# Pooled attention and a top-1 mixture of experts on one core: one last scatter, an early drain of POOL, gathers behind their test, and undivided second tiles

## The chip, the cores and the metric

The kernel runs on one core of one Trainium2 chip. The core has five engines, each with an instruction queue of its own: TensorE (PE in the profile, with PEld for its weight loads), VectorE (DVE), ScalarE (ACT), GpSimd (POOL) and SyncE (SP, which issues most DMAs). POOL issues the indirect DMAs: gathers and scatters of rows by an index per partition. The metric is the device time of one execution in microseconds, the median over several.

## The reference

The inputs are `q`, `k`, `v` of 8 batches x 8 heads x 576 positions x 64, a modality id for each of the 4608 tokens, a gate matrix 512x8, a bias per modality, and the experts' weights `w1` (8 x 512 x 1024) and `w2` (8 x 1024 x 512), all in float32. Cut to what matters:

```python
k_p = k.reshape(B, H, S // 8, 8, D).mean(axis=3); v_p = ...          # pooled by 8
attn = softmax(q @ k_p.T / sqrt(D)) @ v_p
x = attn.transpose(0, 2, 1, 3).reshape(B * S, H * D)                 # 4608 tokens x 512
logits = x @ w_gate + modality_bias[modality_id]
e_idx = argmax(logits); gate_w = softmax(logits)[e_idx]
for e in range(E):                                                    # each token goes to one expert
    mask = e_idx == e
    out[mask] = gate_w[mask, None] * (relu(x[mask] @ w1[e]) @ w2[e])
```

## The kernel before, in words

**Attention.** Tokens are worked on in 36 tiles of 128, in 20 steps of two tiles (`z` = 0 and 1) or one "mixed" tile. The tiles form four groups of nine; groups 0 and 1 are early, 2 and 3 late (`EARLY_GROUPS`). `x_dve` (L603) ends a tile: PSUM tile `av` holds for each head the weighted sum of values and, in a last column, the sum of weights. DVE takes the sums (L620), their reciprocals (L622) and the logits' share (L624), then writes the row `xo` of the tile into `xw` (xb in the profile). An early tile is divided on DVE, in two halves of 256 columns (L626 and L631). A late tile is divided on DVE in its upper half only (L626); ACT copies the lower half as it is (L629), and the reciprocals go into eight further columns of the row (`RX`). SP stores the rows to `xs` in DRAM, where a row has 512 + 16 columns: the token's vector, its gate, and the eight factors, which are 1 for rows that are divided already. `av` has a single buffer, so PE can start the next tile's product only when DVE and ACT have read it. Further small steps of the routing are "dripped" between DVE's instructions (`gap`).

**Experts.** Tokens are sorted by expert into slots of 256 (two tiles of 128). A slot belongs to one expert; the number of slots depends on the data and is 18 to 27 (`NSTAT` to `NSLOT`). Slots 0 and 1 take tokens from the early groups and are prepared during the attention. For each slot:

- POOL gathers its rows from `xs` (`gather`, L141, two indirect DMAs into `xg`), multiplies the lower half of each tile by its factors (`scale_half`, L148, the product at L152), PE transposes the tiles (`x_transposes`, L155, the transposes at L161), ACT and DVE split the result into a high and a low part (L163, L164).
- For `f` in 0 to 7, an eighth of the hidden units: `hidden(f)` is 12 matmuls into `hp` (L170), with ReLU on ACT (L172) and the low part on DVE (L174); `second(f)` is 6 matmuls into `op` (L1155). `renew(f)` splits the next slot's weights: high part on ACT (L136), low part on DVE, a subtraction 128x1024 from two SBUF operands (L139), after which SP loads the weights of the slot after that.
- `evac` (L1132) multiplies `op` by the gate, tile 0 on DVE (L1137), tile 1 on ACT (L1139), and POOL scatters both tiles to `out` (L1141). A scatter waits for the landing of the one before it.

`run` (L1188) writes the order out by hand. In slot s, at `f` = 0 stand `evac` of slot s - 1 (`tail`) and the gather of slot s + 1, at `f` = 3 the factors' product, at `f` = 5 the transposes for slot s + 1; at the end of `f` = 7 the first hidden step of the next slot. Slot 1 differs: its gather is at `f` = 3, the product at 5, the transposes at 6, because the indices of slot 2 are only computed in slots 0 and 1 (`late`, L1103: the table's product and the five DVE steps that finish it, L763 to L767, stand at slot 1, `f` = 2).

**The end.** The number of slots is read into a register in all engines. From slot 17 (`NSTAT` - 1) on, after `f` = 2 (`CUT` = 3), a test decides whether a further slot follows (`more`, L1267, the test at L1280). If it does, the slot is finished by `run`, the next slot's first three steps follow, and so on, nested. If not, `end` or `end_half` (L1222, L1236, chosen by a test at L1272) finishes the slot without preparing another; `end_half` does so when the last slot has only one tile of tokens. On a path that skips DMAs, the POOL queue waits for those in flight and accounts for the skipped ones, so that the semaphores agree where the paths meet (`EVENT_SEMAPHORE` and `INC_SWDGE_SEM` at L1280). `last_rows` (L1215) writes the last rows to `obl[0]` (DVE) and `obl[1]` (ACT); `end_half` sets `obl[1]` to zero, and its indices lie outside of `out`. Behind all tests stand two scatters (L1289), `obl[1]` first. L1317 is the end of the program, with a DRAIN on every engine.

With these inputs 19 slots are used, 0 to 18; slot 18 has one tile and takes `end_half`. The gather of slot 19 that stands at `f` = 0 of slot 18 is issued, and nobody reads it.

Of the kernel before, what the change touches and what calls it, by code (L numbers as in the profile page):

```python
# [12 lines left out]
I32 = mybir.dt.int32  # L13
# [17 lines left out]
def kernel(  # L31
# [116 lines left out]
    def scale_half(s, xgs):  # L148
        for tt in range(2):
            x = xgs[(2 * s + tt) % len(xgs)]  # L150
            xv = x[:, 0:D // 2].rearrange("p (h d) -> p h d", h=H // 2)
            nc.gpsimd.tensor_tensor(xv, xv, x[:, RX:RX + H // 2].rearrange("p (h o) -> p h o", o=1).to_broadcast([P, H // 2, HD]),  # L152
                                    op=ALU.mult)
# [37 lines left out]
    with ExitStack() as actx:  # L191
# [411 lines left out]
        def x_dve(t):  # L603
# [5 lines left out]
            if gi == 0:  # L609
# [7 lines left out]
            late = g >= EARLY_GROUPS  # L617
# [8 lines left out]
            nc.vector.tensor_tensor(xo[:, D // 2:D].rearrange("p (h d) -> p h d", h=4),  # L626
                                    avv[:, 1, :, 0:HD], rb[:, 1].to_broadcast([P, 4, HD]), op=ALU.mult)
            if late:
                nc.scalar.copy(xo[:, 0:D // 2].rearrange("p (h d) -> p h d", h=4), avv[:, 0, :, 0:HD])  # L629
# [495 lines left out]
    def part(s):  # L1125
# [6 lines left out]
        def evac(tts=(0, 1)):  # L1132
            for tt in tts:
                ob = mp.tile([P, D], F32, tag="ob", bufs=4, name=f"ob_{s}_{tt}")
                gt = xg[(2 * s + tt) % 4][:, D:D + 1]
                if tt == 0:
                    nc.vector.tensor_scalar_mul(ob, o[tt], gt)  # L1137
# [3 lines left out]
                nc.gpsimd.indirect_dma_start(  # L1141
                    out=out[:, :], out_offset=IndirectOffsetOnAxis(idx.bitcast(U32), 0),
                    in_=ob, in_offset=None, bounds_check=NTOK - 1, oob_is_err=False)
# [44 lines left out]
        def run(fs, tail):  # L1188
            for f in fs:
# [11 lines left out]
                if s == 1 and f == 3:  # L1201
# [13 lines left out]
        def last_rows(tt):  # L1215
            gt = xg[(2 * s + tt) % 4][:, D:D + 1]
            if tt == 0:
                nc.vector.tensor_scalar_mul(obl[0], o[0], gt)
            else:
                nc.scalar.activation(obl[1], o[1], AF.Copy, scale=gt)  # L1220

        def end(f0):  # L1222

            nc.vector.tensor_copy(sl, sidx[:, 2 * s:2 * s + 2])
# [6 lines left out]
            last_rows(1)  # L1231
            for f in range(f0, NF):
                second(f, (0,), at[f])
            last_rows(0)

        def end_half(f0):  # L1236

            nc.vector.tensor_copy(sl, sidx[:, 2 * s:2 * s + 2])
            nc.vector.memset(obl[1], 0.0)
# [6 lines left out]
            last_rows(0)  # L1246
# [6 lines left out]
    obl = [mp.tile([P, D], F32, name=f"obl{z}") for z in range(2)]  # L1253
    sl = mp.tile([P, 2], I32, name="sl")
# [33 lines left out]
    for tt in (1, 0):  # L1288
        nc.gpsimd.indirect_dma_start(  # L1289
            out=out[:, :], out_offset=IndirectOffsetOnAxis(sl[:, tt:tt + 1].bitcast(U32), 0),  # L1290
            in_=obl[tt], in_offset=None, bounds_check=NTOK - 1, oob_is_err=False)
# [30 lines left out]
```

## Time and profile before

| | us |
|---|---|
| median of 3 runs | 634.19 (633.3 to 634.3) |
| profiled execution | 631.66 |
| its span, first to last instruction | 629.9 |
| PE busy | 601.1 (95%) |
| DVE busy | 409.1 (65%) |
| ACT busy | 347.6 (55%) |
| POOL busy | 237.8 (38%) |

The granted clock of TensorE is 0.992 in the mean. The attention lasts until about 187 us, slot 1 runs from about 198 to 221, slot 18 begins at about 600, PE's last matmul ends at 617.8. A busy share alone says little here; what can be gained is read from the stretches in which PE is idle and from what ends that idle time. In the rows, a time in square brackets is the idle time of the engine ahead of the instruction, followed by what ended it; `x18 | 7.4, 413 |` means 18 instructions, 7.4 us in all, 413 ns each.

### The profile page before, as it was taken

How to read it: one execution, taken by the hardware profiler on the slowest of the kernel's cores; microseconds unless marked ns; L12 is line 12 of the kernel's file. 1: busy time of each engine (PE TensorE's matmuls, PEld its weight loads, DVE VectorE, ACT ScalarE, POOL GpSimd, SP SyncE). 2: the span in 40 equal slices, each digit the busy share in tenths (PEclk: the TensorE clock that was granted, in tenths of full speed). 3: DMA queues.
4: the chain of work that ended last, by engine and by line, in shares of the span. 5: the costliest groups of instructions: out<-in, count | busy, mean ns of one | idle time of the engine just before them, and what ended most of it. 6: DMA issues, size and time to landing. Idle time of an engine off the chain costs nothing.

```text
span 629.9 us, 12488 instructions
## 1 busy us (share of the span) xinstructions
PE 601.1 (95%) x4223; PEld 544.8 (86%) x4223; DVE 409.1 (65%) x802; ACT 347.6 (55%) x666; POOL 237.8 (38%) x326
## 2 busy tenths in 40 slices
PE   4799999999999999999999999999999999999992
PEld 3699888897898898999999999999999999999991
DVE  4767888778957487656656566566566656656641
ACT  2667677887532555555555555555555555555540
POOL 5789968742000341331332331331331241331331
PEclk9899999999999999999999999999999999999997
DMA  9999969864113620120220460120135310120120
GB/s 252 308 284 350 355 199 362 261 209 137 53 70 110 227 69 17 52 69 7 64 69 16 153 223 31 50 68 18 53 91 183 132 56 18 53 69 18 52 70 19
DMA packets 63481, 77.12 MB, mean 122 GB/s; under 512 B 15535, under 2 KB 42159, under 8 KB 63408
## 3 DMA queue, kind: packets, MB, share of 16 engines
q1 hardware_dynamic: 57168, 55.98, 28.2%
q0 software_dynamic: 6240, 20.26, 10.0%
q8 instruction: 35, 0.57, 0.4%
q14 instruction: 38, 0.31, 0.2%
HBM read 119.94 MB, written 19.71 MB: 222 GB/s over the span
## 4 chain that ended last, share of the span: by engine, by line
PE 78%; DMA 6%; DVE 5%; issue 4%; ACT 3%; SPq 1%; POOL 1%; POOLq 0%; ACTq 0%; DVEq 0%
PE op L1155 29%; PE hp L170 29%; PE av L597 5%; PE sc L533 4%; PE av L601 2%; PE xt L161 2%; PE pq L508 2%; DMA out_dram<-ob,sidx 2%; PE pp L562 1%; PE ph L170 1%; DMA xg<-xs,gidx 1%; DMA k<-in_k_dram 1%; DMA raw<-in_moe_w_dram 1%; DVE kp L309 1%; DVE sb L543 1%
## 5 line engine op out<-in xcount | busy, mean ns | idle before, releaser
L136 ACT CAST hl<-raw 128x1024 fp32r<-128x1024 f32 x138 | 144.8, 1049 | 138.7 <-PE op L1155 134.7
L170 PE MATMUL hp<-xh,hl 128*128 128x256 f32 x1152 | 186.1, 284 | 0.0
L170 PEld LDWEIGHTS hp<-xh,hl 128*128 128x128 f32 x1152 | 166.1, 189 | 10.5
L139 DVE TENSOR_TENSOR hl<-raw,hl 128x1024 fp32r<-128x1024 f32 x144 | 175.0, 1217 | 0.0
L1155 PE MATMUL op<-hl,hh 128*128 128x512 f32 x554 | 173.5, 394 | 0.0
L1141 POOL DMA_INDIRECT out_dram<-ob,sidx x36 | 52.5, 1457 | 289.6 <-DVE ob L1137 184.5
L174 DVE SCALAR_TENSOR_TENSOR hlo<-hp,hh 128x256 fp32r<-128x256 f32 x139 | 58.7, 423 | 136.4 <-ACT hh L172 123.8
L1155 PE MATMUL op<-hl,hlo 128*128 128x512 f32 x277 | 108.4, 391 | 0.0
L1155 PEld LDWEIGHTS op<-hl,hh 128*128 128x128 f32 x554 | 94.8, 189 | 12.1
L170 PE MATMUL hp<-xl,hl 128*128 128x256 f32 x576 | 92.0, 282 | 0.0
L172 ACT ACTIVATE hh<-hp 128x256 fp32r<-128x256 f32 x139 | 53.3, 383 | 49.7 <-PE hp L170 47.8
L170 PEld LDWEIGHTS hp<-xl,hl 128*128 128x128 f32 x576 | 79.0, 190 | 0.0
L1155 PEld LDWEIGHTS op<-hl,hlo 128*128 128x128 f32 x277 | 52.0, 188 | 11.7
L597 PE MATMUL av<-vw,pt 128*128 128x146 f32 (+1 forms) x320 | 50.4, 297 | 1.4 <-ACT pt L567 0.9
L143 POOL DMA_INDIRECT xg<-xs,gidx x40 | 44.2, 1105 | 16.5 <-issue 10.4
L152 POOL TENSOR_TENSOR xg<-xg 128x256 f32<-128x256 f32 x34 | 31.2, 918 | 34.9 <-DMA xg<-xs,gidx 34.9
L597 PEld LDWEIGHTS av<-vw,pt 128*128 128x128 f32 (+1 forms) x320 | 40.3, 182 | 3.8 <-ACT pt L567 2.3
L533 PE MATMUL sc<-kt,qt 128*128 128x144 f32 x256 | 38.0, 292 | 0.0
L164 DVE TENSOR_TENSOR xl<-xt,xh 128x512 fp32r<-128x512 f32 x38 | 24.6, 685 | 17.1 <-ACT xh L163 17.1
L533 PEld LDWEIGHTS sc<-kt,qt 128*128 128x128 f32 x256 | 34.2, 195 | 0.2
L540 DVE TENSOR_REDUCE mx<-sc 128x8 f32<-128x576 f32 (+1 forms) x40 | 27.7, 692 | 10.0 <-PE sc L533 8.3
L601 PE MATMUL av<-vw,pt 128*128 128x146 f32 (+1 forms) x160 | 30.7, 295 | 0.4
(236 smaller groups left out, 713.0 us busy)
## 6 DMA issues: line engine op xcount, KB each, us to landing
raw<-in_moe_w_dram SPq DMA_DIRECT2D x304, 256.0 KB
xs<-xb SPq DMA_DIRECT2D x16, 528.0 KB
k<-in_k_dram SPq DMA_DIRECT2D x7, 1024.0 KB
v<-in_v_dram SPq DMA_DIRECT2D x7, 1024.0 KB
q<-in_q_dram SPq DMA_DIRECT2D x6, 1024.0 KB
q<-in_q_dram SPq DMA_DIRECT2D x4, 512.0 KB
v<-in_v_dram SPq DMA_DIRECT2D x16, 128.0 KB
xs<-xb SPq DMA_DIRECT2D x8, 132.0 KB
```

The costliest lines, as they stand in the source:

```text
L136: nc.scalar.copy(hl[f][:, 0, :], raw[f])
L139: eng.tensor_sub(hl[f][:, 1, :], raw[f], hl[f][:, 0, :].bitcast(F32))
L143: nc.gpsimd.indirect_dma_start(out=xgs[(2 * s + tt) % len(xgs)], out_offset=None, in_=xs[0:rows, :], in_offset=IndirectOffsetOnAxis(idx[:, ...
L152: nc.gpsimd.tensor_tensor(xv, xv, x[:, RX:RX + H // 2].rearrange("p (h o) -> p h o", o=1).to_broadcast([P, H // 2, HD]), op=ALU.mult)
L170: nc.tensor.matmul(ph, hl[f][:, w, d * P:(d + 1) * P], x[:, d, :], start=(n == 0 and d == 0), stop=(n == 2 and d == ND - 1))
L172: nc.scalar.activation(hh, ph, AF.Relu)
L174: nc.vector.scalar_tensor_tensor(hlo, ph, 0.0, hh.bitcast(F32), op0=ALU.max, op1=ALU.subtract)
L533: nc.tensor.matmul(dst, qt[:, i, :], kt[b % NB][:, :, h * SPL:(h + 1) * SPL], start=True, stop=True)
L597: nc.tensor.matmul(av[hs, u, 2 * VC * gg:2 * VC * (gg + 1)], pt[:, c, hs], vw[y][:, c].rearrange("p a x -> p (a x)"), start=(gg == 0), sto ...
L601: nc.tensor.matmul(dst4[hs], pt4[:, hs], v4[y][:, 2 * u:2 * u + 2, :], start=False, stop=True)
L1141: nc.gpsimd.indirect_dma_start(out=out[:, :], out_offset=IndirectOffsetOnAxis(idx.bitcast(U32), 0), in_=ob, in_offset=None, bounds_check=N ...
L1155: nc.tensor.matmul(o[tt], l[:, ts_], hl[f][:, w, D:2 * D], start=(f == 0 and n == 0), stop=(f == NF - 1 and n == 2))
```

## The change

- `scale_half` becomes `scale`: POOL multiplies all 512 columns of both tiles, not 256.
- In `x_dve` only second tiles (`z` = 1) of the late groups leave undivided, and they do so whole: one copy 128x512 on ACT, nothing on DVE. First tiles and mixed tiles of the late groups are divided on DVE in two halves, as the early ones are.
- In slot 1 the two scatters of slot 0's rows are put off (`later`) until behind the product for slot 2; slot 2's gather moves from `f` = 3 to `f` = 2, its product from 5 to 4.
- From slot 17 on, the gather of the next slot moves from `f` = 0, ahead of the test, to `f` = 3, behind it; the product moves from 3 to 4, the transposes from 5 to 6.
- In slot 16, at `f` = 4, behind the product for slot 17, POOL gets a `drain`.
- There is one scatter behind all tests. `end` scatters its second tile itself, through `evac`; the first tile, or the only one, is multiplied by the gate half on DVE and half on ACT and goes out by the one last scatter. `end_half` no longer sets a second tile to zero.

```diff
-    def scale_half(s, xgs):
+    def scale(s, xgs):
...
-            xv = x[:, 0:D // 2].rearrange("p (h d) -> p h d", h=H // 2)
-            nc.gpsimd.tensor_tensor(xv, xv, x[:, RX:RX + H // 2].rearrange("p (h o) -> p h o", o=1).to_broadcast([P, H // 2, HD]),
+            xv = x[:, 0:D].rearrange("p (h d) -> p h d", h=H)
+            nc.gpsimd.tensor_tensor(xv, xv, x[:, RX:RX + H].rearrange("p (h o) -> p h o", o=1).to_broadcast([P, H, HD]),
...
-            late = g >= EARLY_GROUPS
+            late = g >= EARLY_GROUPS and z == 1
...
-            nc.vector.tensor_tensor(xo[:, D // 2:D].rearrange("p (h d) -> p h d", h=4),
-                                    avv[:, 1, :, 0:HD], rb[:, 1].to_broadcast([P, 4, HD]), op=ALU.mult)
             if late:
-                nc.scalar.copy(xo[:, 0:D // 2].rearrange("p (h d) -> p h d", h=4), avv[:, 0, :, 0:HD])
+                nc.scalar.copy(xo.rearrange("p (u h d) -> p u h d", u=2, h=4), avv[:, :, :, 0:HD])
             else:
-                nc.vector.tensor_tensor(xo[:, 0:D // 2].rearrange("p (h d) -> p h d", h=4),
-                                        avv[:, 0, :, 0:HD], rb[:, 0].to_broadcast([P, 4, HD]), op=ALU.mult)
+                for u in range(2):
+                    nc.vector.tensor_tensor(xo[:, u * D // 2:(u + 1) * D // 2].rearrange("p (h d) -> p h d", h=4),
+                                            avv[:, u, :, 0:HD], rb[:, u].to_broadcast([P, 4, HD]), op=ALU.mult)
...
                 if f == 0:
-                    tail()
-                    if nxt and s >= EARLY_SLOTS:
+                    if s == 1:
+                        tail(later=later)
+                    else:
+                        tail()
+                    if nxt and EARLY_SLOTS <= s < NSTAT - 1:
                         gather(s + 1, gidx, 2 * (s + 1), xg)
...
-                if s == 1 and f == 3:
+                if s == 1 and f == 2:
+                    gather(s + 1, gidx, 2 * (s + 1), xg)
+
+                if s >= NSTAT - 1 and f == CUT and nxt:
                     gather(s + 1, gidx, 2 * (s + 1), xg)
...
-                if f == (5 if s == 1 else 3) and nxt and not early:
-                    scale_half(s + 1, xg)
-                if f == (6 if s == 1 else 5) and nxt:
+                if f == (3 if EARLY_SLOTS <= s < NSTAT - 1 else 4) and nxt and not early:
+                    scale(s + 1, xg)
+                    while later:
+                        later.pop(0)()
+                if s == NSTAT - 2 and f == 4:
+                    nc.gpsimd.drain()
+                if f == (5 if EARLY_SLOTS <= s < NSTAT - 1 else 6) and nxt:
                     x_transposes(s + 1, xg)
...
+        def last_rows():
+
+            gt = xg[2 * s % 4][:, D:D + 1]
+            nc.vector.tensor_scalar_mul(obl[:, 0:D // 2], o[0][:, 0:D // 2], gt)
+            nc.scalar.activation(obl[:, D // 2:D], o[0][:, D // 2:D], AF.Copy, scale=gt)
...
-            last_rows(1)
+            evac((1,))
             for f in range(f0, NF):
                 second(f, (0,), at[f])
-            last_rows(0)
+            last_rows()
...
-            nc.vector.memset(obl[1], 0.0)
...
-    for tt in (1, 0):
-        nc.gpsimd.indirect_dma_start(
-            out=out[:, :], out_offset=IndirectOffsetOnAxis(sl[:, tt:tt + 1].bitcast(U32), 0),
-            in_=obl[tt], in_offset=None, bounds_check=NTOK - 1, oob_is_err=False)
+    nc.gpsimd.indirect_dma_start(
+        out=out[:, :], out_offset=IndirectOffsetOnAxis(sl.bitcast(U32), 0),
+        in_=obl, in_offset=None, bounds_check=NTOK - 1, oob_is_err=False)
```

More of the change, by code (lines that the diff above doesn't have):

```diff
@@ L1130, in part, with evac @@
         early = s + 1 < EARLY_SLOTS
-        def evac(tts=(0, 1)):
+        def evac(tts=(0, 1), later=None):
             for tt in tts:
@@ L1140, in evac, with put @@
                 idx = (sidx0 if s < EARLY_SLOTS else sidx)[:, 2 * s + tt:2 * s + tt + 1]
-                nc.gpsimd.indirect_dma_start(
-                    out=out[:, :], out_offset=IndirectOffsetOnAxis(idx.bitcast(U32), 0),
-                    in_=ob, in_offset=None, bounds_check=NTOK - 1, oob_is_err=False)
+                def put(ob=ob, idx=idx):
+                    nc.gpsimd.indirect_dma_start(
+                        out=out[:, :], out_offset=IndirectOffsetOnAxis(idx.bitcast(U32), 0),
+                        in_=ob, in_offset=None, bounds_check=NTOK - 1, oob_is_err=False)
+                if later is None:
+                    put()
+                else:
+                    later.append(put)
         def hidden(f, at=None):
@@ L1188, in run @@
         def run(fs, tail):
+            later = []
             for f in fs:
@@ L1192, in run @@
                 if f == 0:
-                    tail()
-                    if nxt and s >= EARLY_SLOTS:
+                    if s == 1:
+                        tail(later=later)
+                    else:
+                        tail()
+                    if nxt and EARLY_SLOTS <= s < NSTAT - 1:
                         gather(s + 1, gidx, 2 * (s + 1), xg)
@@ L1213, in run @@
                     renew(f)
[L1215 to L1220, printed above, removed]
+        def last_rows():
+            gt = xg[2 * s % 4][:, D:D + 1]
+            nc.vector.tensor_scalar_mul(obl[:, 0:D // 2], o[0][:, 0:D // 2], gt)
+            nc.scalar.activation(obl[:, D // 2:D], o[0][:, D // 2:D], AF.Copy, scale=gt)
         def end(f0):
-            nc.vector.tensor_copy(sl, sidx[:, 2 * s:2 * s + 2])
+            nc.vector.tensor_copy(sl, sidx[:, 2 * s:2 * s + 1])
             at = {f: hx[f - f0] for f in range(f0, NF)}
@@ L1230, in end @@
             second(NF - 1, (1,), at[NF - 1])
-            last_rows(1)
+            evac((1,))
             for f in range(f0, NF):
                 second(f, (0,), at[f])
-            last_rows(0)
+            last_rows()
         def end_half(f0):
-            nc.vector.tensor_copy(sl, sidx[:, 2 * s:2 * s + 2])
-            nc.vector.memset(obl[1], 0.0)
+            nc.vector.tensor_copy(sl, sidx[:, 2 * s:2 * s + 1])
             at = {f: hx[f - f0] for f in range(f0, NF)}
@@ L1245, in end_half @@
             second(NF - 1, (0,), at[NF - 1])
-            last_rows(0)
+            last_rows()
         return slot0 if s == 0 else run, end, evac, end_half
@@ L1251 @@
     hx = [[mp.tile([P, SLOT], F32R, name=f"hx{i}_{z}") for z in range(2)] for i in range(NF - CUT)]
-    obl = [mp.tile([P, D], F32, name=f"obl{z}") for z in range(2)]
-    sl = mp.tile([P, 2], I32, name="sl")
+    obl = mp.tile([P, D], F32, name="obl")
+    sl = mp.tile([P, 1], I32, name="sl")
     lag = []
```

2 lines of the change are left out of this document (1 added, 1 removed).

## The prediction

> **What bounds the kernel now.** I read first the busy time by stage, to see where TensorE (PE) is not the bound. Columns: stretch, its length, then busy us and instructions of PE, weight loads, DVE, ACT, POOL, the granted clock, DMA share and GB/s.
>
> ```profile
> 90.00:187.00 97.00, 94.31 (x788) 86.03 (x787) 75.88 (x228) 66.19 (x183) 39.59 (x62) 1.00 0.59 191
> 218.00:578.00 360.00, 360.00 (x2363) 327.74 (x2364) 225.81 (x308) 197.24 (x291) 104.11 (x90) 1.00 0.21 68
> 618.00:630.00 12.00, 0.00 (x0) 0.00 (x0) 0.61 (x1) 0.00 (x0) 1.92 (x2) 0.69 0.07 23
> ```
>
> From 218 to 578 PE has no idle time, so nothing can be won there; things can only be lost. What is to be won lies in three places: 2.69 us of idle PE in the late attention (97.00 less 94.31), one wait at slot 1, and 12 us at the end in which PE does nothing. The waits of PE name the first two, and the waits of ACT one more:
>
> ```profile
> PE xt L161 <- ACT qt L514: 1.0, 1, 1.0
> PE xt L161 <- POOL xg L152: 0.7, 1, 0.7
> ACT xb L629 <- DVE xb L626: 8.9, 8, 2.2
> ```
>
> The third place I read in the timeline of the last microseconds, in the chain of waits that ends last (start, length, what), and in the instructions of two lines (L1280 is the slot test, L1317 the end of the program; three numbers are min/median/max in ns, then first and last start):
>
> ```profile
> 616.22 1.60 PE L1155 MATMUL op<-hl,hx 128*128 128x512 f32 x6
> 617.86 0.75 DVE L1218 TENSOR_SCALAR obl<-op,xg 128x512 f32<-128x512 f32 x1 [0.60 <-PE op L1155]
> 617.91 1.01 POOL L1289 DMA_INDIRECT out_dram<-obl,sl  x1 [8.62 <-DVE hx L174]
> 621.63 1.00 POOL L1289 DMA_INDIRECT out_dram<-obl,sl  x1 [2.71 <-DMA out_dram<-obl,sl]
> ```
> ```profile
> 614.31 2.54 issue
> ...
> 617.91 2.94 DMA out_dram<-obl,sl
> ```
> ```profile
> L1280 POOLq EVENT_SEMAPHORE  x5: 17/43/5426, 606.7 to 612.5; - x5
> L1280 POOLq INC_SWDGE_SEM  x1: 1699/1699/1699, 612.5 to 612.5; - x1
> ```
> ```profile
> L1317 SPq DRAIN  x3: 7/7/13, 624.9 to 629.4; - x3
> L1317 POOLq DRAIN  x3: 40/113/7685, 621.4 to 629.7; - x3
> ```
>
> The rows to publish are ready at 618.61 (617.86 + 0.75), yet their scatter starts at 621.63: POOL first sends the scatter of the other tile (617.91) and waits 2.71 for its landing. Then POOL sits in a DRAIN from 621.4 to 629.1 (621.4 + 7.685), while SP, which waits for every DMA, is through at 624.9. So of the 12 us some 3 are one scatter behind another, and some 4 are POOL alone, after all data has landed.
>
> **The change, part by part.** The span is 629.9 us, the profiled execution 631.66; the unprofiled ones have a median of 634.19 (633.3 to 634.3). I work out a difference in the profile and take it off the median.
>
> *One last scatter.* Removed: one of the two scatters, a memset and half of the DVE product, which is split between DVE and ACT. The halves are 128x256; the nearest rows of that size:
>
> ```profile
> L626 DVE TENSOR_TENSOR xb<-av,xb 128x256 f32<-128x256 f32 x18 | 7.4, 413 | 0.0
> L629 ACT COPY xb<-av 128x256 f32<-128x256 f32 x18 | 6.7, 372 | 17.4 <-DVE xb L626 8.9 <-PE sc L533 3.3 <-PE pq L508 2.9
> ```
>
> So the rows are ready at about 617.86 + 0.41 = 618.27. At the start of slot 18 stands the same pair, DVE product then scatter:
>
> ```profile
> 600.21 0.74 DVE L1137 TENSOR_SCALAR ob<-op,xg 128x512 f32<-128x512 f32 x1
> 601.24 1.77 POOL L1141 DMA_INDIRECT out_dram<-ob,sidx  x1 [10.40 <-DVE ob L1137]
> ```
>
> It has 0.29 between them (600.21 + 0.74 to 601.24).
>
> The one scatter therefore starts at about 618.6 in place of 621.63: 3.0 us. It costs nothing only if POOL is there by then. Before, POOL spent 5.43 at the test on landings (the gather of slot 19 among them, which nobody reads, and which now moves behind the test), 1.70 on INC_SWDGE_SEM, and came to the scatter's line at 616.85, after 2.54 of issue time behind its last branch. Now it has no such gather to wait for; I give it back one more 1.70 and one more 2.54, because the scatter that the full ending now holds has to be accounted for where it is skipped: still about 617. From the other side, were none of the wait saved, POOL would come at 616.85 + 1.70 + 2.54 = 621.1 and the gain of 3.0 would shrink to 0.5. I take 3.0, since the wait has lost its cause.
>
> *The drain in slot 16.* The closing DRAIN takes 7.685; the two after it, with nothing new to finish, 0.113 and 0.040. So the instruction costs next to nothing by itself and the long one works something off. Only part is the last scatter: this lands about 2.8 after its start (2.94 for the scatter before it), at 624.4, and POOL needs 4.7 more. The groups of POOL's indirect DMAs:
>
> ```profile
> L1141 POOL DMA_INDIRECT out_dram<-ob,sidx x36 | 52.5, 1457 | 289.6 <-DVE ob L1137 184.5 <-ACT hh L172 85.8 <-PE op L1155 10.3
> L143 POOL DMA_INDIRECT xg<-xs,gidx x40 | 44.2, 1105 | 16.5 <-issue 10.4 <-DVE t0lo L766 4.6 <-PE hp L170 0.9
> ```
>
> With the 2 of L1289 they are 78, and no drain stands among them. If the 4.7 are book-keeping over these, 0.06 each, a drain in slot 16 leaves the last one 7 (two scatters and two gathers of slot 17, two scatters of slot 18, the last): 0.4 in place of 4.7, a gain of up to 4.3. If they are a fixed price behind any indirect DMA, the gain is 0. I take 4.2, because the end is then held by SP, 0.5 behind the landing (624.9 less 624.4). The trace shows no drain in the middle; the two short DRAINs, with an empty backlog, are the rows nearest to what the last one would become. On its own place the drain is covered, by the idle time of POOL ahead of slot 17's first scatter:
>
> ```profile
> 578.61 1.78 POOL L1141 DMA_INDIRECT out_dram<-ob,sidx  x1 [12.29 <-DVE ob L1137]
> ```
>
> POOL idles 12.29 us there, and even the whole 7.685 from 566.3 (578.61 less 12.29) ends at 574.0. Uncovered it would hold up the scatters of slot 17 and, behind them, its gathers.
>
> The Trainium skill (VectorE: DVE Perf Modes, The DRAIN you can't avoid) speaks against this gain: it calls the DRAINs of a program's preamble and postamble boilerplate of about 12 ns, constant, on all engines. SP's rows agree (7 to 13 ns), POOL's 7685 does not; by that page an extra drain takes nothing away, and the sum is the first rival's.
>
> *Slot 2's gather first.* In slot 1 POOL issues two scatters of slot 0, the second behind the landing of the first, and only then the gathers:
>
> ```profile
> 204.46 0.17 DVE L765 TENSOR_SCALAR gidx<-t4ix 128x6 int32<-128x6 f32 x1
> 208.34 1.47 POOL L1141 DMA_INDIRECT out_dram<-ob,sidx  x1 [5.86 <-DMA raw<-in_moe_w_dram]
> 210.12 1.04 POOL L143 DMA_INDIRECT xg<-xs,gidx  x1 [0.30 <-DMA raw<-in_moe_w_dram]
> 216.27 1.60 POOL L152 TENSOR_TENSOR xg<-xg 128x256 f32<-128x256 f32 x1 [1.12 <-DMA xg<-xs,gidx]
> 217.93 0.66 PE L161 MATMUL xt<-ident,xg 128*128 128x128 f32 x4 [0.71 <-POOL xg L152]
> ```
>
> The indices are there at 204.63, so the first gather can start near 204.9, 5.2 us earlier. By the same interval as before (216.27 less 210.12) the second product starts near 211 and, doubled and held up, ends by 213.5, ahead of the 217.2 at which PE asks. PE's 0.71 goes, and nothing else is late there. The two scatters move behind the products, to about 214 and, by the same 6.9 between them as before (the first began at 201.42), 221, still ahead of the next slot's:
>
> ```profile
> 201.42 1.05 POOL L1141 DMA_INDIRECT out_dram<-ob,sidx  x1 [51.24 <-ACT hh L172]
> ...
> 224.67 1.77 POOL L1141 DMA_INDIRECT out_dram<-ob,sidx  x1 [6.79 <-DVE ob L1137]
> ```
>
> Gain 0.7; without the move ahead it would be a loss, as the doubled products would end 0.5 to 1 us later than the 217.9 of before.
>
> *Undivided second tiles.* In each pair of late attention tiles DVE does two halves for the first and none for the second, ACT one whole copy for the second: the sum for DVE is the same but for two mixed tiles, 2 x 0.41. ACT's copy stood behind DVE's half (8.9 us over 8 of them) and now needs only the reciprocal. PE waits little for ACT here; the one wait of 1.0 has such a copy in ACT's queue ahead of it, 0.37 of work. Bounds: gain up to that 1.0, loss up to the 0.82 of DVE; I take a gain of 0.3.
>
> *The price of it:* POOL multiplies 128x512 per tile in place of 128x256, in every slot, where PE has no idle time.
>
> ```profile
> L152 POOL TENSOR_TENSOR xg<-xg x34: 607/614/1665, 214.5 to 590.2; 128x256 f32<-128x256 f32 x34
> L304 POOL TENSOR_TENSOR v<-v x23: 724/1264/1289, 12.9 to 136.4; 128x512 f32<-128x512 f32 x15, 128x256 f32<-128x256 f32 x8
> ```
>
> Alone a half takes 0.61; the fold goes from 0.72 to 1.26 for twice the width, so a whole one takes about 1.07, 1.2 at most. The tightest slot I find:
>
> ```profile
> 494.35 1.22 DVE L139 TENSOR_TENSOR hl<-raw,hl 128x1024 fp32r<-128x1024 f32 x1
> 495.38 0.65 POOL L152 TENSOR_TENSOR xg<-xg 128x256 f32<-128x256 f32 x1 [1.76 <-DMA xg<-xs,gidx]
> 496.72 0.61 POOL L152 TENSOR_TENSOR xg<-xg 128x256 f32<-128x256 f32 x1 [0.68 <-DMA xg<-xs,gidx]
> 497.61 1.03 PE L161 MATMUL xt<-ident,xg 128*128 128x128 f32 x8
> ```
>
> The first product now ends by 496.5 (behind DVE's subtraction, which ends at 495.57), the second starts with its data at 496.72 and ends at 497.8; PE takes that tile after half of its 1.03, at about 498.1. It holds by 0.3. POOL in turn holds up DVE:
>
> ```profile
> 330.40 1.51 DVE L139 TENSOR_TENSOR hl<-raw,hl 128x1024 fp32r<-128x1024 f32 x1
> 332.88 0.42 DVE L174 SCALAR_TENSOR_TENSOR hlo<-hp,hh 128x256 fp32r<-128x256 f32 x1 [0.97 <-ACT hh L172]
> ```
>
> Here a product began first, L139 took 1.51 in place of 1.22, and DVE still idled 0.97 before its next step. A whole product holds it up by at most 1.07, against the 1.26 that DVE idles undisturbed (0.97 + 0.29). Cost 0.
>
> *Gather behind the test.* In slot 17 gather and transposes both move:
>
> ```profile
> 584.79 1.04 POOL L143 DMA_INDIRECT xg<-xs,gidx  x1 [0.30 <-PE hp L170]
> 591.30 1.03 PE L161 MATMUL xt<-ident,xg 128*128 128x128 f32 x8
> ```
>
> The gather already came late, behind the second scatter (584.79), the transposes ran at 591.30 and now come one step later (18 of the 2363 matmuls in 360.00 us: 2.7 us), so there is room for the 2 x 0.6 that the doubled products add. Cost 0; if the gather itself came 2 us later, still 0.
>
> Sum: 3.0 + 4.2 + 0.7 + 0.3 = 8.2 us, so 634.2 - 8.2 = 626.0.
>
> **The rivals.** *The drain shortens nothing.* POOL's 4.7 are a fixed tail; for it speaks that one profile can't tell fixed from accumulated. Gain 3.0 + 0.7 + 0.3 = 4.0: 630.2. The page of the Trainium skill named above would give the same.
>
> *The end does not move.* POOL comes to its last scatter as late as before, through branches and accounting, or the DRAIN ends by something that I don't see. Left are 0.7 + 0.3 and at most 0.5: about 633.0 to 633.2, no change that can be measured (a measurement of this kernel tells about 0.2%, 1.3 us).
>
> *Slower: the doubled product outlasts its slack.* Place: the transposes of each slot from 2 on. If a whole product takes 2.2 us alone, not 1.07, then in the slot above the chain 495.57 + 2.0 + 2.0 ends at 499.6, PE waits 1.5; five slots have this rhythm (7.5 us), the others have some 2 us of slack before it reaches PE. From about 0.6 lost in each of 15 slots on, the loss passes the gain of 8.2; at 0.7 in each of them it is 10.5, and the time 636.5. Against it: the slowest of the 34 halves took 1.67, waiting included.
>
> **How the numbers follow.** Forecast, all four gains: 0.62. Drain without effect: 0.25. End unmoved: 0.07. Slower: 0.06. The range runs from 624.6 (1.0 in the attention, POOL a little earlier) to 631.2 (the first rival with 1 us less); it leaves out the last two cases and some 0.05 on the fast side. Faster 0.62 + 0.25 = 0.87, same 0.07, slower 0.06.
>
> **What would show it.** One scatter at the end, starting about 0.3 after DVE's half; a closing DRAIN of about 3 in place of 7.7, and a long one near 566 to 574; no wait of PE for POOL xg in slot 1 or later; POOL's product near 1.07 alone; PE still without idle time from 218 to 578. I am wrong if the closing DRAIN still lasts 4 or 5 us beyond the landing, if POOL reaches its last scatter after 619, or if PE's transposes begin to wait for POOL.

## The result, and the profile after

| | before | after | predicted |
|---|---|---|---|
| median, us | 634.19 (5 runs, 632.4 to 634.3) | 625.37 (5 runs, 624.1 to 627.3) | 626.0 (624.6 to 631.2) |
| ratio, 95% interval | | 0.9871 (0.985 to 0.9893) | 0.987 |
| profiled execution, us | 631.66 | 627.34 | |
| its span, us | 629.9 | 625.5 | |

The medians fell by 8.8 us, the two profiled spans by 4.4 only. Where they differ can be read by cutting both traces at instructions that both have. The cuts are the first late tile's L620, the last tile's L620, the first matmul of `second` in slot 0, the transposes for slot 3, those for slot 17, PE's last matmul, the end.

| stretch, us | before | after | difference |
|---|---|---|---|
| start to the first late tile (code unchanged) | 104.83 | 108.47 | +3.64 |
| late attention | 78.83 | 77.97 | -0.86 |
| slot 0 to the transposes for slot 3 | 53.25 | 52.35 | -0.90 |
| transposes for slot 3 to those for slot 17 | 329.72 | 329.86 | +0.14 |
| PE's last matmul to the end (the tail) | 12.12 | 5.70 | -6.42 |

The first stretch isn't touched by the change. In the profiles of the experiments below, where its code is the same, it takes anything from 104.9 to 108.9. That, and that after's profile is of the slowest of its five executions, is why the two spans show less than the medians do. The other stretches repeat within 0.1 in kernels that share their code (slots 3 to 17 of after are 0.14 longer than in the others, of which more below), the tail within 0.3, so they are what the experiments are judged by. What the table leaves out, from the last late tile to slot 0 and from slot 17 to PE's last matmul, is the same in both kernels (1.23 and 49.95). The gains are 0.86 + 0.90 + 6.42 = 8.18 us, or 8.04 with the 0.14 taken off.

The timeline of after's last microseconds (start, length, instruction, idle time before it and what ended it):

```profile
618.23 1.60 PE L1160 MATMUL op<-hl,hx 128*128 128x512 f32 x6
...
619.87 0.48 DVE L1234 TENSOR_SCALAR obl<-op,xg 128x256 f32<-128x256 f32 x1 [0.60 <-PE op L1160]
620.39 0.47 ACT L1235 ACTIVATE obl<-op,xg 128x256 f32<-128x256 f32 x1 [1.57 <-DVE obl L1234]
621.14 0.97 POOL L1302 DMA_INDIRECT out_dram<-obl,sl  x1 [12.55 <-ACT obl L1235]
```

One scatter is left and it waits for its rows, not for another scatter. It starts 1.3 us behind PE, where the last one before started 3.8 behind. But the two halves run one behind the other: ACT's was released by DVE's. The instructions of the end's line and of the drain's and the test's lines (min/median/max in ns, first and last start):

```profile
L1330 POOLq DRAIN  x3: 46/112/3485, 620.9 to 625.3; - x3
L1330 SPq DRAIN  x3: 7/7/13, 624.6 to 624.9; - x3
```
```profile
L1223 POOLq DRAIN  x1: 7793/7793/7793, 567.3 to 567.3; - x1
```
```profile
L1294 POOLq INC_SWDGE_SEM  x1: 279/279/279, 610.4 to 610.4; - x1
```

The closing DRAIN lasts 3.485 in place of 7.685 and is over at 624.4, just before SP is through (624.6). The long one now lies in slot 16, from 567.3 to 575.1. INC_SWDGE_SEM, 1.699 before, takes 0.28.

Slot 1 and the tightest slot, POOL beside the PE and DVE rows that matter:

```profile
207.26 0.17 DVE L764 TENSOR_SCALAR gidx<-t4ix 128x6 int32<-128x6 f32 x1
...
208.18 1.04 POOL L143 DMA_INDIRECT xg<-xs,gidx  x1 [53.80 <-DMA raw<-in_moe_w_dram]
...
216.19 2.09 POOL L152 TENSOR_TENSOR xg<-xg 128x512 f32<-128x512 f32 x1 [0.73 <-DMA xg<-xs,gidx]
218.45 1.05 POOL L1142 DMA_INDIRECT out_dram<-ob,sidx  x1 [0.16 <-POOL xg L152]
...
219.43 0.82 PE L161 MATMUL xt<-ident,xg 128*128 128x128 f32 x6
```
```profile
498.90 1.04 POOL L152 TENSOR_TENSOR xg<-xg 128x512 f32<-128x512 f32 x1 [0.56 <-DMA xg<-xs,gidx]
499.04 1.98 DVE L139 TENSOR_TENSOR hl<-raw,hl 128x1024 fp32r<-128x1024 f32 x1
499.25 0.40 PE L1160 MATMUL op<-hl,hlo 128*128 128x512 f32 x1
499.48 1.17 PE L161 MATMUL xt<-ident,xg 128*128 128x128 f32 x8
```

The gather now stands ahead of the scatters, right behind the indices, and PE takes the tiles at 219.43 without a wait. In the tightest slot a whole product takes 1.04 and ends at 499.94. The second tile's transposes begin at 500.00 (inside the row at 499.48). That is no margin: the weight load of that tile waited for POOL, and the four transposes ahead of it, which take 0.43 in every other slot, take 0.52.

```profile
500.00 0.42 PEld L161 LDWEIGHTS xt<-ident,xg 128*128 128x128 f32 x4 [0.16 <-POOL xg L152]
```

From these transposes to those for the next slot it takes 23.55 in place of 23.41, the whole 0.14 of the table. In the nine other profiles that have the whole product once, the tile is ready 0.10 to 0.57 ahead here, and at most 0.02 is lost. DVE's subtraction, which began after the product, takes 1.98. The busy time of the stretch doesn't show the 0.14, PE counts as busy throughout; the other two rows are the subtraction and the product as groups:

```profile
218.00:578.00 360.00, 360.00 (x2363) 327.50 (x2362) 230.62 (x308) 197.84 (x291) 116.43 (x93) 1.00 0.22 70
```
```profile
L139 DVE TENSOR_TENSOR hl<-raw,hl 128x1024 fp32r<-128x1024 f32 x144 | 179.4, 1247 | 0.0
L152 POOL TENSOR_TENSOR xg<-xg 128x512 f32<-128x512 f32 x34 | 45.0, 1326 | 31.4 <-DMA xg<-xs,gidx 31.3
```

### The profile page after: what moved, and what is told of

Its sections match the earlier page's. It is cut to its first block, busy times and chain, and to the rows that moved or that the text cites. A ratio compares the mean times of both kernels' runs of the same rounds, so it can differ in the third digit from the quotient of the medians.

```text
span 625.5 us, 12457 instructions
## 1 busy us (share of the span) xinstructions
PE 601.5 (96%) x4223; PEld 545.5 (87%) x4223; DVE 414.8 (66%) x803; ACT 347.6 (56%) x657; POOL 245.8 (39%) x323
## 4 chain that ended last, share of the span: by engine, by line
PE 80%; DVE 7%; issue 4%; POOL 3%; DMA 3%; ACT 1%; SPq 0%; POOLq 0%; DVEq 0%; ACTq 0%
PE op L1160 31%; PE hp L170 30%; PE av L597 5%; PE sc L533 3%; PE xt L161 2%; PE av L601 2%; PE pq L508 2%; PE pp L562 2%; PE ph L170 1%; DMA out_dram<-ob,sidx 1%; DMA k<-in_k_dram 1%; DVE sb L543 1%; POOL v L304 1%; DVE mx L540 1%; DVE kp L309 1%
## 5 line engine op out<-in xcount | busy, mean ns | idle before, releaser
L139 DVE TENSOR_TENSOR hl<-raw,hl 128x1024 fp32r<-128x1024 f32 x144 | 179.4, 1247 | 0.0
L170 PEld LDWEIGHTS hp<-xh,hl 128*128 128x128 f32 x1152 | 166.1, 189 | 10.5
L1142 POOL DMA_INDIRECT out_dram<-ob,sidx x36 | 50.4, 1400 | 226.4 <-DVE ob L1136 175.4
L143 POOL DMA_INDIRECT xg<-xs,gidx x38 | 41.5, 1092 | 69.3 <-DMA raw<-in_moe_w_dram 53.8
L152 POOL TENSOR_TENSOR xg<-xg 128x512 f32<-128x512 f32 x34 | 45.0, 1326 | 31.4 <-DMA xg<-xs,gidx 31.3
```

Of the source, the lines that this page charges most:

```text
L139: eng.tensor_sub(hl[f][:, 1, :], raw[f], hl[f][:, 0, :].bitcast(F32))
L143: nc.gpsimd.indirect_dma_start(out=xgs[(2 * s + tt) % len(xgs)], out_offset=None, in_=xs[0:rows, :], in_offset=IndirectOffsetOnAxis(idx[:, ...
L152: nc.gpsimd.tensor_tensor(xv, xv, x[:, RX:RX + H].rearrange("p (h o) -> p h o", o=1).to_broadcast([P, H, HD]), op=ALU.mult)
L170: nc.tensor.matmul(ph, hl[f][:, w, d * P:(d + 1) * P], x[:, d, :], start=(n == 0 and d == 0), stop=(n == 2 and d == ND - 1))
L1142: nc.gpsimd.indirect_dma_start(out=out[:, :], out_offset=IndirectOffsetOnAxis(idx.bitcast(U32), 0), in_=ob, in_offset=None, bounds_check=N ...
```

## The experiments

My theory is the prediction's sum: the drain works off a backlog that would else end the program, the single scatter takes the other's landing out of the end, slot 1's gather and the attention give the rest, and the doubled product is covered. Each edit below is against the kernel after, unless it says otherwise. Line numbers shift by a few. "Slots 1 to 3" and "slots 3 to 17" are the third and fourth stretch of the table above.

| run | median, us | ratio to before, interval | late attention | slots 1 to 3 | slots 3 to 17 | tail |
|---|---|---|---|---|---|---|
| no_drain | 629.64 | 0.9925 (0.9898 to 0.9951) | 77.96 | 52.35 | 329.72 | 9.35 |
| drain_slot8 | 625.24 | 0.987 (0.9847 to 0.9894) | 77.98 | 52.35 | 329.72 | 6.75 |
| before_drain | 630.15 | 0.9935 (0.9912 to 0.9959) | 78.83 | 53.25 | 329.72 | 8.06 |
| two_last | 626.96 | 0.9893 (0.9868 to 0.9919) | 77.97 | 52.35 | 329.72 | 8.12 |
| old_slot1 | 626.22 | 0.9865 (0.9837 to 0.9894) | 77.97 | 54.14 | 329.68 | 5.74 |
| slot1_f3 | 624.58, one run | | 77.95 | 52.37 | 329.74 | 5.43 |
| old_halves | 626.86 | 0.9881 (0.9855 to 0.9908) | 78.84 | 52.35 | 329.72 | 5.43 |
| product_twice | 663.46 | 1.0479 (1.0423 to 1.0536) | 77.98 | 52.79 | 363.11 | 5.44 |
| gather_ahead | 627.0, one run | | 77.94 | 52.37 | 329.72 | 5.43 |
| last_act | 625.7 | 0.9861 (0.9838 to 0.9884) | 77.93 | 52.35 | 329.72 | 5.99 |
| last_act_b (the same kernel) | 624.19, one run | | 77.96 | 52.35 | 329.72 | 5.78 |
| last_dve | 624.48, one run | | 77.99 | 52.35 | 329.72 | 5.18 |

**no_drain: the drain taken out.**

```diff
-                if s == NSTAT - 2 and f == 4:
-                    nc.gpsimd.drain()
```

> The changed kernel without its drain in slot 16. Backlog theory: the closing DRAIN works off every indirect DMA since the last drain, so it lasts 4 to 4.5 us beyond the landing of the last scatter again (0.3 in the changed kernel), the account at the slot test (INC_SWDGE_SEM, 0.28 in the changed kernel) takes 1.7 again, and the time is 4 us above the changed kernel's 625.4: about 629.5. Rival, a drain does nothing and the tail is fixed: DRAIN and INC_SWDGE_SEM stay short, the time stays near 625.4, and the short tail came from somewhere else in the change.

The rows of its end and of its test:

```profile
L1328 POOLq DRAIN  x3: 40/113/7427, 620.3 to 628.3; - x3
L1328 SPq DRAIN  x3: 7/7/13, 623.8 to 628.0; - x3
```
```profile
L1292 POOLq INC_SWDGE_SEM  x1: 1639/1639/1639, 609.8 to 609.8; - x1
```

The tail grows by 9.35 - 5.70 = 3.65, and the closing DRAIN is back at 7.4, though there is one scatter only. SP had been ready for it at 623.8. So the drain in slot 16 shortens the end. INC_SWDGE_SEM is back too.

**drain_slot8: the drain in the middle.** A fixed first-time price, paid once by whichever drain comes first, would look the same as a backlog in no_drain. A drain with fewer DMAs ahead of it tells them apart.

```diff
-                if s == NSTAT - 2 and f == 4:
+                if s == 8 and f == 4:
```

> The changed kernel with its drain in slot 8 in place of slot 16. Backlog theory: eight slots more, four indirect DMAs each, are left to the closing DRAIN: 32 x 0.06 = 1.9 us longer, so it ends about 2.2 us beyond the landing, of which SP hides 0.6; the time is about 1.5 us above the changed kernel (627.0), and INC_SWDGE_SEM lies between 0.28 and 1.7, near 0.8. Rival, what counts is that a drain was there at all (a first-time price): closing DRAIN, INC_SWDGE_SEM and time as in the changed kernel.

```profile
L1330 POOLq DRAIN  x3: 46/113/4822, 617.2 to 622.6; - x3
L1330 SPq DRAIN  x3: 7/7/13, 621.0 to 622.3; - x3
```
```profile
L1294 POOLq INC_SWDGE_SEM  x1: 919/919/919, 606.7 to 606.7; - x1
```

With about half of the DMAs behind the drain, the closing one takes 4.8, between 3.5 and 7.4, and outlasts SP's readiness by 1.0 (617.2 + 4.822 against 621.0). INC_SWDGE_SEM lies between as well, 0.92 against 0.28 and 1.64. A first-time price would have left 3.5. The tail is 1.05 longer, not 1.5 as expected; the median, 625.24, can't tell that from the kernel after.

The backlog could still be of time, not of DMAs. The two drains in mid-program tell these apart. Each starts while POOL's last product is at work, so what it takes by itself is counted from the end of that product. The product and the drain here, then the product in after, whose drain is shown above:

```profile
376.54 2.20 POOL L152 TENSOR_TENSOR xg<-xg 128x512 f32<-128x512 f32 x2 [1.67 <-DMA xg<-xs,gidx]
```
```profile
L1223 POOLq DRAIN  x1: 4122/4122/4122, 377.7 to 377.7; - x1
```
```profile
566.46 3.03 POOL L152 TENSOR_TENSOR xg<-xg 128x512 f32<-128x512 f32 x2 [1.84 <-DMA xg<-xs,gidx]
```

The drain in slot 8 starts at 377.66 unrounded and runs 3.04 us past the product, with 36 indirect DMAs before it; the one in slot 16 starts at 567.34 and runs 5.65 past it, with 68, as in every other run that has it. That is 0.084 and 0.083 us per DMA, while the second stands only 1.5 times as late in the program. Where no drain stands ahead of it, the closing DRAIN fits too: from the end of the last scatter it runs 6.46 us in the kernel before (78 DMAs) and 6.22 in no_drain (75), again 0.083 each. INC_SWDGE_SEM grows by 0.020 for each: 0.279, 0.919 and 1.639 with 6, 38 and 74 DMAs since the last drain. So it is the DMAs that count. Only the closing DRAIN of drain_slot8 is 0.4 longer than 39 of them would make it (3.61 past its scatter), which stays open.

**before_drain: the kernel before with the drain and nothing else.**

```diff
+                if s == NSTAT - 2 and f == 4:
+                    nc.gpsimd.drain()
```

> The kernel before with nothing but the drain in slot 16. Backlog theory: 4.2 us faster than before (634.2 to about 630.0), closing DRAIN under 0.6 us beyond the landing, INC_SWDGE_SEM 0.3, and still two scatters one behind the other at the end. Rival, the drain does nothing by itself: 634.2, unchanged within 0.2%.

```profile
621.12 1.01 POOL L1291 DMA_INDIRECT out_dram<-obl,sl  x1 [7.79 <-ACT hx L172]
625.40 1.00 POOL L1291 DMA_INDIRECT out_dram<-obl,sl  x1 [3.26 <-DMA out_dram<-obl,sl]
```

The tail falls by 12.12 - 8.06 = 4.06 by the drain alone. The two last scatters stand 0.74 ahead of and 3.53 behind PE's last matmul. In the kernel before the first stood 0.09 behind it: by the rows POOL itself came late there (616.85), and the shorter INC_SWDGE_SEM brings it in time; here ACT's `hx` releases it.

**two_last: two last scatters, as before, with everything else of the change** (`last_rows(tt)`, both `obl`, the loop over two scatters taken back).

> The changed kernel with the two last scatters of before (the first of rows outside of the output, the second behind its landing; the last product whole on DVE). My theory: the second scatter starts 3.0 us later again relative to PE's last matmul (3.8 in place of 1.3 us behind it), so the time is 2.5 to 3 us above the changed kernel: about 628. Rival, POOL is in time now and sends the empty scatter well before the end, since the wait at the slot test is shorter: the second one starts as soon as its product is ready, 1.05 us behind PE, and the time is that of the changed kernel or 0.3 less.

```profile
615.96 0.97 POOL L1305 DMA_INDIRECT out_dram<-obl,sl  x1 [10.51 <-ACT hx L172]
620.34 0.97 POOL L1305 DMA_INDIRECT out_dram<-obl,sl  x1 [3.41 <-issue]
```

The tail is 8.12, so the single scatter is worth 2.42. A rival for this run had been that a POOL in time sends the empty scatter so early that it costs nothing. It falls: the scatter stands behind ACT's last `hx`, 0.74 ahead of PE's end, and the second one still starts 4.38 after it. The change can be taken apart in two orders: from before the drain first gives 4.06 and the rest 2.36, the single scatter first (no_drain) 2.77 and then the drain 3.65. Both add up to 6.42 because they start and end at the same kernels; what they show is that neither part changes by more than 0.41 with the order.

**old_slot1: slot 1 in the old order, with the doubled product.**

```diff
-                    if s == 1:
-                        tail(later=later)
-                    else:
-                        tail()
+                    tail()
...
-                if s == 1 and f == 2:
+                if s == 1 and f == 3:
...
-                if f == (3 if EARLY_SLOTS <= s < NSTAT - 1 else 4) and nxt and not early:
+                if f == (5 if s == 1 else 3 if s < NSTAT - 1 else 4) and nxt and not early:
```

> The changed kernel with slot 1 as before: both scatters of slot 0 ahead of the gather, gather at f = 3, product at f = 5 (whole tiles, as in the changed kernel). My theory: POOL's order decides; the gather comes some 5 us later relative to PE, the doubled products end behind PE's demand, and PE waits 1.2 to 1.8 us for POOL at the transposes of slot 2. From the first second() of slot 0 to the transposes for slot 3 it takes 53.5 to 54.2 us, against 53.25 before and 52.35 in the changed kernel; the time is about 626.8. Rival, the 0.9 us that these slots gained have another cause: 52.35 and 625.4 again.

The waits of PE from 190 to 400 us:

```profile
PE xt L161 <- POOL xg L152: 1.3, 1, 1.3
```

The stretch takes 54.14, 1.79 more than after and 0.89 more than before. The doubled product alone would have cost slot 1 0.9, as the prediction's last sentence on this part has it (0.5 to 1).

**slot1_f3: the scatters put off, gather and product at the old places in the order** (only the last two edits of old_slot1).

> Slot 1 with the two scatters still put off, but its gather back at f = 3 and its product at 5. My theory (only what stands ahead of the gather in POOL's queue counts, and that is the same): gather at about 208.2 relative to the profile after, no wait of PE for xg, slots 1 to 3 in 52.3 to 52.4 us. Rival (the earlier place is needed too): the gather or the product comes later by up to one step of 2.7 us, and the stretch takes 52.6 to 54.

```profile
204.88 0.17 DVE L764 TENSOR_SCALAR gidx<-t4ix 128x6 int32<-128x6 f32 x1
...
205.80 1.04 POOL L143 DMA_INDIRECT xg<-xs,gidx  x1 [53.82 <-DMA raw<-in_moe_w_dram]
```

The rows are DVE's, which writes the indices, and POOL's first gather. The indices were ready at 205.05, so the gather starts 0.75 behind them, as in after (208.18 against 207.43). The stretch is the same, 52.37. All of the gain comes from what POOL does ahead of the gather; the move by one `f` is worth nothing. (My expected start of 208.2 was that of after's profile; this one was 2.4 us earlier throughout.)

**old_halves: both late tiles undivided in their lower half, and the half product, as before.**

```diff
-            xv = x[:, 0:D].rearrange("p (h d) -> p h d", h=H)
+            xv = x[:, 0:D // 2].rearrange("p (h d) -> p h d", h=H // 2)
...
-            late = g >= EARLY_GROUPS and z == 1
+            late = g >= EARLY_GROUPS
...
-                nc.scalar.copy(xo.rearrange("p (u h d) -> p u h d", u=2, h=4), avv[:, :, :, 0:HD])
+                nc.scalar.copy(xo[:, 0:D // 2].rearrange("p (h d) -> p h d", h=4), avv[:, 0, :, 0:HD])
```

> The changed kernel with the late tiles as before: both tiles of a pair divided in the upper half on DVE and copied in the lower half on ACT, POOL multiplying halves. My theory: the late attention (from the first late tile's L620 to the last tile's) takes 78.8 us again, 0.86 more than in the changed kernel; slots 3 to 17 take 329.72 us in either form, since the doubled product costs PE nothing; the time is about 626.2. Rival, the doubled product does cost something in the slots: slots 3 to 17 get shorter than 329.72 and the time falls below 625.4.

Its waits of PE in the late attention:

```profile
PE xt L161 <- ACT qt L514: 1.0, 1, 1.0
PE av L597 <- ACT pt L567: 0.9, 3, 0.3
```

The late attention is back at 78.84, and so is the wait of 1.0 that before had and after hasn't. What PE waits for is ACT's copy of `qt` (L514). In the kernel before it stood in ACT's queue behind the copy of an undivided half. That one started 0.08 behind DVE's half of the tile (done at 154.47), with ACT idle for 1.85 ahead of it, though `pq` was ready for the copy behind it at 153.03:

```profile
154.55 0.37 ACT L629 COPY xb<-av 128x256 f32<-128x256 f32 x1 [1.85 <-PE pq L508]
154.81 0.59 ACT L514 COPY qt<-pq 128x512 f32<-128x512 f32 x1
```

In after this tile is one that DVE divides whole, ACT has no copy of it, and PE doesn't wait. Slots 3 to 17 take 329.72 with the half product, as with the whole one in the runs above.

**product_twice: a second whole product per tile.** This tests the slower rival, whose condition was 2.2 us of product per tile.

```diff
+            nc.gpsimd.tensor_tensor(xq.rearrange("p (h d) -> p h d", h=H), xv, x[:, RX:RX + H].rearrange("p (h o) -> p h o", o=1).to_broadcast([P, H, HD]),
+                                    op=ALU.mult)
             nc.gpsimd.tensor_tensor(xv, xv, x[:, RX:RX + H].rearrange("p (h o) -> p h o", o=1).to_broadcast([P, H, HD]),
```

> In front of every product of POOL stands a second one of the same size into a scratch tile that nobody reads, so that a tile costs POOL at least 2.1 us (2 x 1.04, the shortest whole product of the kernel after), the condition of the slower rival. My theory (the slots have little slack for POOL: 0.05 us in the slot at 494 to 500 us): with 1.04 more per tile the second tile comes some 2 us too late in the slots of that rhythm, PE waits for POOL's xg there by 1 to 2 us each, in about five slots, less or not at all in the others; slots 3 to 17 take 334 to 340 us in place of 329.7, the median is 630 to 637. Rival (PE's order of work has room that the trace does not show, or DVE's waiting sets the rhythm): no wait of PE for xg, slots 3 to 17 stay at 329.7 to 330.5, the median at 625 to 626.5.

The waits of PE, and POOL in the slot at 390 us (L152 is the added product, L154 the real one):

```profile
PE xt L163 <- POOL xg L154: 26.2, 15, 3.9
```
```profile
390.88 1.19 POOL L152 TENSOR_TENSOR xq<-xg 128x512 f32<-128x512 f32 x1 [1.64 <-DMA xg<-xs,gidx]
392.15 1.05 POOL L154 TENSOR_TENSOR xg<-xg 128x512 f32<-128x512 f32 x1
393.15 2.02 POOL L152 TENSOR_TENSOR xq<-xg 128x512 f32<-128x512 f32 x1
395.25 1.04 POOL L154 TENSOR_TENSOR xg<-xg 128x512 f32<-128x512 f32 x1
```

The mechanism is the rival's, and far dearer than I expected: 33 us in slots 3 to 17, not 4 to 10. PE waits not in five slots but in 14 of the 15, 1.1 to 3.9 us a time. In the kernel after the second tile is ready 0.05 to 2.6 us ahead of PE in these slots, about 1.5 in half of them; the added products, held up by DVE like the 2.02 above, bring it some 3 us later. The waits explain 23.5 of the 33.4 in that stretch; most of the rest is the clock (last section).

**gather_ahead: the gather of a further slot ahead of its test again.**

```diff
-                    if nxt and EARLY_SLOTS <= s < NSTAT - 1:
+                    if nxt and s >= EARLY_SLOTS:
                         gather(s + 1, gidx, 2 * (s + 1), xg)
...
-                if s >= NSTAT - 1 and f == CUT and nxt:
-                    gather(s + 1, gidx, 2 * (s + 1), xg)
```

> The changed kernel with the gathers from slot 17 on ahead of the test again, so that slot 19 is gathered and not read. My theory: POOL comes to the last scatter's line 2 to 4 us later than in the changed kernel (613.4, 6.4 us before PE's last matmul), since it waits for the landings of that gather, but still before PE's end, so that the tail stays 5.7 us: this edit gains nothing by itself. Rival, it is what makes the early arrival, and without it the last scatter starts later than 1.30 us behind PE and the tail is 6.5 or more.

The chain that ended last in this kernel, and in after:

```profile
603.25 11.51 DMA out_dram<-ob,sidx
...
617.44 0.04 POOLq L1300
```
```profile
603.25 7.36 DMA out_dram<-ob,sidx
...
613.40 0.04 POOLq L1302
```

POOL comes to its last scatter at 617.44 in place of 613.40, and still 2.4 ahead of PE's end (6.4 in after). The scatter starts at +1.31, as in after. So this part of the change made room that nothing here uses.

**last_act and last_act_b: the last product whole on ACT. last_dve: whole on DVE.**

```diff
-            nc.vector.tensor_scalar_mul(obl[:, 0:D // 2], o[0][:, 0:D // 2], gt)
-            nc.scalar.activation(obl[:, D // 2:D], o[0][:, D // 2:D], AF.Copy, scale=gt)
+            nc.scalar.activation(obl, o[0], AF.Copy, scale=gt)
```

In last_dve the added line is `nc.vector.tensor_scalar_mul(obl, o[0], gt)`.

> The changed kernel with the last product whole on ACT in place of half on DVE and half on ACT. In the changed kernel ACT's half began only when DVE's was done, so the rows were ready 1.03 us behind PE's last matmul and the scatter started at 1.30. My theory: whole on ACT, 0.68, they are ready at about 0.75 and the scatter starts at 1.0, so the tail from PE's last matmul to the end is 5.4 in place of 5.70 us; in the time 0.3 us can't be told. Rival, the two halves overlapped in effect, and whole on ACT is no earlier or later: tail 5.7 or more.

> The last product whole on ACT, once more. Scatter again at +1.00 after PE's last matmul. If the long landing of the first time (3.52) was chance, it now takes 2.7 to 3.0 and the tail is 5.3 to 5.6 us; if it belongs to this kernel (what lies beside the scatter at that instant), again about 3.5 and a tail near 6.0.

> The last product whole on DVE, nothing on ACT. My theory (the two halves of the kernel after run one behind the other, so that the split costs and does not save): rows ready 0.78 us behind PE's last matmul in place of 1.03, scatter at +1.05 to +1.10 in place of +1.30, and with a landing of 2.7 to 3.0 a tail of 5.4 to 5.6 us. Rival (the wait of ACT's half for DVE's is an accident of that run): scatter at +1.3 or later, tail 5.7 or longer.

The last rows of last_act and of last_dve:

```profile
619.04 0.69 ACT L1234 ACTIVATE obl<-op,xg 128x512 f32<-128x512 f32 x1 [1.07 <-PE op L1160]
620.00 0.97 POOL L1301 DMA_INDIRECT out_dram<-obl,sl  x1 [12.26 <-ACT obl L1234]
```
```profile
617.63 0.75 DVE L1234 TENSOR_SCALAR obl<-op,xg 128x512 f32<-128x512 f32 x1 [0.60 <-PE op L1160]
618.65 0.98 POOL L1301 DMA_INDIRECT out_dram<-obl,sl  x1 [12.29 <-DVE obl L1234]
```

Unsplit, the scatter starts at +1.00 on ACT and +1.06 on DVE, in place of +1.30. On DVE that reaches the end: a tail of 5.18 with a landing 2.6 behind the scatter's start, against 5.43 in the runs that keep the split and have a landing of 2.6 to 2.7 too (old_halves, slot1_f3). On ACT the landing took 3.5 and 3.3 in the two runs, so nothing is won. In both an instruction fetch by DMA began 1.53 to 1.56 after the scatter, just when its packets start; in last_dve and after there was none between 0.7 and 2.3. That goes with the longer landing, but no run forced it, so the cause stays open. The 0.25 of last_dve is 0.04%, which no median here can confirm.

## Why the prediction was right

The time, the sign and the mechanism hold: 8.0 to 8.2 us by the stretches and 8.8 by the medians against 8.2 predicted. The terms hold less well than their sum: the two at the end fell short, the two before came out larger, and that these misses nearly cancel is luck.

- *One last scatter*: 3.0 predicted, 2.4 (two_last) to 2.8 (no_drain against before) found. The step that failed is "So the rows are ready at about 617.86 + 0.41 = 618.27", 0.45 behind PE's last matmul: it takes the halves to run side by side, but ACT's waited for DVE's, the rows were ready 1.03 behind, and a whole product on DVE (0.75) is quicker (last_dve). The 0.29 from product to scatter was right (0.28: 620.39 + 0.47 to 621.14). POOL was there in time, as taken.
- *The drain in slot 16*: 4.2 predicted, 3.65 to 4.06 found. It is a backlog: beyond SP's last wait the closing DRAIN ran 3.9 us with no drain (620.3 + 7.427 - 623.8), 1.0 with one in slot 8, nothing with one in slot 16. The first rival, no effect, is refuted. The size of a piece was too small: 0.06 comes of counting only what lies behind the landing (4.7 / 78), but the DRAIN works beside the landing, from the scatter's end on, at 0.083 each. That the drain in slot 16 delays nothing was right: from the transposes for slot 17 to PE's last matmul it takes 49.95 us with it (after) and without (no_drain).
- The Trainium skill (VectorE: DVE Perf Modes, The DRAIN you can't avoid) has the DRAINs of a program's start and end as a constant of about 12 ns on all engines. SP's rows are near it (7 to 13 ns), POOL's closing DRAIN behind indirect DMAs takes 3.2 to 7.7 us in these runs. So the rule, by which the early drain would have gained nothing, doesn't hold for POOL here.
- INC_SWDGE_SEM was taken as a fixed 1.70, and I counted one more of it. It belongs to the same backlog (1.64, 0.92, 0.28). That the drain also brings POOL in time was not foreseen.
- *Slot 2's gather first*: 0.7 predicted, 0.90 found. The gather went 4.7 us ahead in place of 5.2: it started at 208.18, 0.75 behind its indices, not 0.3. After's trace runs 2.8 us later there (indices at 207.43 in place of 204.63); with that taken off, the second product ended at 215.5, not by 213.5, since the gathers landed 6.0 and 6.6 us after their start in place of 4.4 and 4.7. PE came to the transposes at 216.6, so that didn't matter.
- *The attention*: 0.3 predicted from a range of -0.82 to 1.0, 0.86 found. The wait of 1.0 is gone, and 0.86 of it is left as a gain; I took too little of the bound that had a named wait behind it. By the rows it went because that tile has no copy on ACT any more, not because a copy now needs only the reciprocal.
- *The doubled product*: cost 0 predicted; 0 in nine profiles with it, 0.14 in after's own. Alone it takes 1.04 (1.07 predicted). In after's tightest slot the margin of 0.3 is gone, because the second product starts 0.58 ahead of PE's first transposes there (498.90 to 499.48); the prediction took the 0.89 of before (496.72 to 497.61), and the second gather landed 4.5 us after its start in place of 4.2. So one sign of being wrong that the prediction named, transposes that wait for POOL, did show, for 0.14 of some 8 us. The slower rival was priced too low: its condition, run in product_twice, costs 38 us and not 10.5, since products and subtractions hold each other up, the other slots have about 1.5 us to spare and not 2, and the clock falls.
- *Gather behind the test*: cost 0, right, and gain 0, as its cover was not needed once INC_SWDGE_SEM was short.
- In the second rival, 1.0 and at most 0.5 off 634.2 leave 632.7 to 633.2, not 633.0 to 633.2; nothing hangs on it.

## What to carry to other kernels

A POOL that has issued many indirect DMAs owes work which it pays at its next drain, here 0.083 us for each, and the end of the program is such a drain: look whether the closing DRAIN outlasts SP's, and put an earlier one where POOL idles long. At the end of a kernel count how many dependent DMAs stand in a row behind the last matmul, and split a short last product over two engines only if the trace shows the halves side by side. A step with "no cost" is safe only by its margin in the tightest repetition: measure it with the step doubled.

## What the runs showed of the hardware that was not expected

**The clock falls after an idle PE.** In product_twice, PE's waits of 1.1 to 1.7 us left the granted clock at 1.00; those of 2.4 and 3.9 us were each followed by about 3.4 to 4 us at half. Four stretches of PE after a wait: the two after the wait of 2.45 us that ended at 396.35, the one after 3.89 us that ended at 242.88, and the one after 1.32 us that ended at 553.57 (stretch, length, PE busy, granted clock, DMA share, GB/s):

```profile
396.35:397.35 1.00, 1.00 (x9) 1.00 0.00 0
397.35:400.75 3.40, 3.40 (x15) 0.53 0.00 0
```
```profile
242.88:246.88 4.00, 4.00 (x18) 0.50 0.00 0
...
553.57:556.97 3.40, 3.40 (x23) 1.00 0.02 5
```

From its transposes to those for the next slot, a slot with a wait of 2.45 us takes 27.65 to 27.75 us in place of 23.4, so 1.8 to 1.9 beyond the wait; the one with 3.89 loses 2.0 beyond its waits; the slots with 1.1 to 1.7 lose 0.2 to 0.3. The four slots with half clock lose 7.5 us in slots 3 to 17 in this way, on top of the 23.5 of waits.

The Trainium skill (TensorE: Matmul & The Clock Gate, HAM oscillation — how this bites in real kernels) tells of this falling clock for gaps longer than about 3.4 us. In product_twice all five of 2.44 us and more did it, and none of the nine up to 1.73. But the length of one wait can't be the whole rule: in the attention of the kernel after, two waits of 0.86 and 0.50 close together, which left PE busy for 2.08 of 3.44 us, were followed by 3.4 us at half. What decides stays open.

```profile
68.00:71.44 3.44, 2.08 (x17) 1.00 1.05 330
71.44:74.85 3.41, 3.41 (x15) 0.50 1.04 389
```

**A backlog of POOL.** INC_SWDGE_SEM and DRAIN on POOL grow with the indirect DMAs since the last drain, not with the time since: 0.28 us for INC_SWDGE_SEM with 6, 0.92 with 38, 1.64 with 74; a drain in mid-program runs 3.04 us past POOL's last work with 36 and 5.65 with 68. With 7 the closing DRAIN (3.2 to 4.1 us) ends about 0.3 behind the last scatter's landing.

**POOL and DVE hold each other up.** The prediction named this; its size is new. The doubled product stretched DVE's subtraction L139 from 175.0 to 179.4 us in sum, single ones from 1.22 to 1.98, and was itself held up to 2.1 in place of 1.04. That cost PE nothing but the 0.14 us above.
